# One PSUM accumulator for x, attention and FFN, and another order of the last loads, in a one-token attention and FFN kernel

## The chip, the cores and the metric

The kernel runs on one core of one Trainium2 chip. The metric is the device time of the program in microseconds (us), taken over several executions. A core has a matmul engine (PE, whose weight loads are listed as PEld), a vector engine (DVE), an activation engine (ACT), and a queue processor (SP), which here issues all loads. Sixteen DMA engines carry them out. PE's clock is granted by a throttle and takes two values in these traces, 1.0 and 0.5 of full speed.

All executions quoted here are fast (none was over 1.5% above the fastest of its kernel).

## The reference, cut to what matters

```python
xn = layernorm(x)                                  # x: 4 x 1 x 640, bf16
q  = xn @ wq                                       # 32 heads of 192
scores = q . k_cache[:, :, -2048:, :] * 192**-0.5  # per batch and head
o  = softmax(scores) . v_cache[:, :, -2048:, :]
attention = o @ wo
ffn = (silu(xn @ w1) * (xn @ w3)) @ w2
return x + attention + ffn                         # 4 x 1 x 640
```

K and V of the window are 32 heads x 3.15 MB each, and every byte is used once. With the weights this is 223 MB of loads for an output of 5 KB.

## The kernel before

The kernel walks through 128 slots, four for each head `h`. In each slot DVE multiplies a quarter of the head's K tile by q, PE sums the products in groups with identity matmuls, and DVE reduces what is left. The softmax of a head follows some slots later, then P·V (`pv`), then a regrouping by small matmuls (`ge_tr`, tile `gp`) and, once for four heads, the product with a tile of wo (`ge_proj`). A list of (slot, phase) entries gives every engine its program order. SP issues the loads in that order too, and waits in that order. K tiles have two buffers, V tiles three.

```python
for h in range(H):
    u0, ul = h * GQ, h * GQ + GQ - 1                                  # GQ = 4, H = 32
    if h >= KBUFS:
        add((h - KBUFS + 1) * GQ, 0, load_k, h)                       # K31: slot 120
    add((h - VBUFS) * GQ + GQ + L, 0, load_v, h, 1 if h < H - 1 else 2)   # V29: slot 118
    for u in range(u0, ul + 1):
        add(u, 1, mult, u)                # DVE
        add(u + 1, 2, adder, u)           # PE
        add(u + 2, 4, reduce_quarter, u)  # DVE
    add(u0 + L, 3, pv, h, 0)              # L = 10
    add(u0 + L + 2, 3, pv, h, 1)
    ...                                   # cut: softmax, regrouping
for hg in range(NG):                      # NG = 8 groups of four heads
    a = ((hg + 1) * HG - 1) * GQ + L + 5
    add((hg - 1) * HG * GQ + L + 2 * GQ + 4 if hg > 0 else 0, 0, wo_load, hg)   # wo7: slot 118
    add(a, 3, ge_proj, hg, 0, RPP // 2)
    add(a + 1, 3, ge_proj, hg, RPP // 2, RPP)
...                                       # cut: the FFN up to h, done in the first third
add(NU + 2, 1, w2_load)                   # two pieces, after slot 128
```

The attention is summed in PSUM over all heads (`acc0` with 512 columns, `acc1` with 128). After the last slot the FFN gets its own pair of accumulators, and three addends are joined outside PSUM:

```python
for c, w2 in enumerate(ffn.pop("w2")):    # 12 chunks
    nc.tensor.matmul(f0[:], lhsT=hT[:, c, :], rhs=w2[:, 0:N0], ...)     # 512 columns
    nc.tensor.matmul(f1[:], lhsT=hT[:, c, :], rhs=w2[:, N0:D], ...)     # 128 columns
nc.vector.tensor_copy(out=attn_bf[:, 0:N0], in_=acc0[:])
nc.vector.tensor_copy(out=attn_bf[:, N0:D], in_=acc1[:])
nc.vector.tensor_tensor(out=t1[:], in0=x_sb[:], in1=attn_bf[:], op=ALU.add)
nc.scalar.copy(out=ffn_bf[:, 0:N0], in_=f0[:])
nc.scalar.copy(out=ffn_bf[:, N0:D], in_=f1[:])
nc.vector.tensor_tensor(out=res[:], in0=t1[:], in1=ffn_bf[:], op=ALU.add)
```

Of the kernel before, what the change touches and what calls it, by code (L numbers as in the profile page):

```python
# [10 lines left out]
FP32 = mybir.dt.float32  # L11
BF16 = mybir.dt.bfloat16
ALU = mybir.AluOpType
# [5 lines left out]
def kernel(  # L19
# [20 lines left out]
    nc = tc.nc  # L40
    P = 128
    B, Sq, D = A_x.shape
    _, H, Sk, Dh = A_k_cache.shape
# [3 lines left out]
    FC = F // P  # L47
    PB = P // B
    NJ = W // PB
    GQ = 4  # L50
# [4 lines left out]
    NG = H // HG  # L55
    CT = 32
    QW = HG * Dh
    RPP = QW // P
    NU = H * GQ
    N0 = 512  # L60
    N1 = D - N0
    QC = 512
    NQ = H * Dh // QC
    assert D % P == 0 and F % QC == 0 and P % B == 0 and W % (PB * GQ) == 0
    assert JQ * DD == 512 and JQ % 2 == 0 and 2 * Dh <= 512 and 0 < N1 <= 512
    assert (H * Dh) % QC == 0 and NQ % 6 == 0 and QW % P == 0 and Dh % RPP == 0 and P == HG * CT
    assert 2 * H * Dh <= NJ * Dh

    ctx.enter_context(tc.manual_schedule())
    const = ctx.enter_context(tc.tile_pool(name="const", bufs=1))  # L70
    fpool = ctx.enter_context(tc.tile_pool(name="ffn", bufs=1))
    kpool = ctx.enter_context(tc.tile_pool(name="kt", bufs=KBUFS))
    vpool = ctx.enter_context(tc.tile_pool(name="vt", bufs=VBUFS))
    ppool = ctx.enter_context(tc.tile_pool(name="pr", bufs=PBUFS))
# [4 lines left out]
    ps_m = ctx.enter_context(tc.tile_pool(name="ps_m", bufs=1, space=MemoryType.PSUM))  # L79
    ps_t = ctx.enter_context(tc.tile_pool(name="ps_t", bufs=1, space=MemoryType.PSUM))  # L80
# [28 lines left out]
    x_sb = const.tile([B, D], BF16, name="x_sb")  # L109
# [3 lines left out]
    for k0 in range(0, KC, 2):  # L113
        n = min(2, KC - k0)
        wt = vpool.tile([P, 2, H * Dh], BF16, tag="vt")
        nc.sync.dma_start(out=wt[:, 0:n, :].rearrange("p k n -> p (k n)"),
                          in_=wq_v[:, k0:k0 + n, :].rearrange("p k n -> p (k n)"))
# [4 lines left out]
    idb = const.tile([P, P], BF16, name="idb")  # L122
# [44 lines left out]
    for c0 in range(0, NQ, 6):  # L167
        qps = [pool.tile([P, QC], FP32, tag=tag, name="qps")
               for pool, tag in ((ps_add, "ps"), (ps_add, "ps"), (ps_o, "o_ps"), (ps_o, "o_ps"), (ps_m, "mt"), (ps_t, "t"))]
        for kc in range(KC):  # L170
            for i, qp in enumerate(qps):
                nc.tensor.matmul(qp[:], lhsT=xnT[:, kc].rearrange("p a b -> p (a b)"),  # L172
                                 rhs=wq_rows[kc][:, (c0 + i) * QC:(c0 + i + 1) * QC],
                                 start=(kc == 0), stop=(kc == KC - 1))
# [13 lines left out]

    acc0 = ps_acc.tile([B, N0], FP32, name="acc0")
    acc1 = ps_acc.tile([B, N1], FP32, name="acc1")  # L190

    def mult(u):
        h, g = u // GQ, u % GQ
        pr = ppool.tile([P, JQ, Dh], BF16, tag="pr")
        nc.vector.tensor_tensor(out=pr[:], in0=kts[h][:, g * JQ:(g + 1) * JQ, :],  # L195
                                in1=qbc[:, h * Dh:(h + 1) * Dh].unsqueeze(1).to_broadcast([P, JQ, Dh]),
                                op=ALU.mult)
        prs[u] = pr
        if g == GQ - 1:
            kts.pop(h)  # L200
# [98 lines left out]
    def ge_proj(hg, i0, i1):  # L299
        oT, wo_t = oTs[hg], wos[hg]  # L300
        for i in range(i0, i1):
            st = (hg == 0 and i == 0)
            sp = (hg == NG - 1 and i == RPP - 1)
            nc.tensor.matmul(acc0[:], lhsT=oT[:, i, :], rhs=wo_t[:, i * D:i * D + N0], start=st, stop=sp)  # L304
            nc.tensor.matmul(acc1[:], lhsT=oT[:, i, :], rhs=wo_t[:, i * D + N0:(i + 1) * D], start=st, stop=sp)  # L305

    h_sb = const.tile([B, F], BF16, name="h_sb")
    hT = const.tile([P, FC, B], BF16, name="hT")
    g_bf = const.tile([B, F], BF16, name="g_bf")
    ffn = {}  # L310
# [28 lines left out]
        nc.vector.tensor_copy(out=hT[:], in_=hT_ps[:])  # L339

    w2_v = B_w2.rearrange("(p c) n -> p c n", c=FC)
    W2A = (2 * FC) // 3

    def w2_load():
        wa = fpool.tile([P, W2A, D], BF16, tag="w", name="w2a")
        nc.sync.dma_start(out=wa[:].rearrange("p c n -> p (c n)"), in_=w2_v[:, 0:W2A, :].rearrange("p c n -> p (c n)"))
        wb = kpool.tile([P, FC - W2A, D], BF16, tag="kt", name="w2b")
        nc.sync.dma_start(out=wb[:].rearrange("p c n -> p (c n)"), in_=w2_v[:, W2A:FC, :].rearrange("p c n -> p (c n)"))
        ffn["w2"] = [wa[:, c, :] for c in range(W2A)] + [wb[:, c, :] for c in range(FC - W2A)]

    sched = defaultdict(list)

    def add(slot, phase, fn, *args):
        sched[slot].append((phase, len(sched[slot]), fn, args))

    for h in range(H):
        u0, ul = h * GQ, h * GQ + GQ - 1
        if h >= KBUFS:
            add((h - KBUFS + 1) * GQ, 0, load_k, h)
        add((h - VBUFS) * GQ + GQ + L, 0, load_v, h, 1 if h < H - 1 else 2)  # L360
        for u in range(u0, ul + 1):
            add(u, 1, mult, u)
            add(u + 1, 2, adder, u)
            add(u + 2, 4, reduce_quarter, u)
        add(u0 + L, 3, pv, h, 0)
        add(u0 + L + 2, 3, pv, h, 1)
        add(ul + 2, 5, chain_lmax, h)
        add(ul + 3, 4, chain_tr, h)
        add(ul + 4, 5, chain_gmax, h)
        add(ul + 5, 4, chain_bc, h)  # L370
        add(ul + 6, 5, chain_z, h)
        add(ul + 6, 4, ge_tot, h)
        add(ul + 6, 6, ge_norm, h)
        add(u0 + L + 3, 3, ge_tr, h)
        add(u0 + L + 4, 5, ge_copy, h)
    for hg in range(NG):
        a = ((hg + 1) * HG - 1) * GQ + L + 5
        add((hg - 1) * HG * GQ + L + 2 * GQ + 4 if hg > 0 else 0, 0, wo_load, hg)
        add(a, 3, ge_proj, hg, 0, RPP // 2)
        add(a + 1, 3, ge_proj, hg, RPP // 2, RPP)  # L380
    f = FFN_HEAD * GQ
# [4 lines left out]
    add(f + 12, 7, ffn_up)  # L386
    add(f + 13, 7, ffn_h)
    add(f + 15, 7, ffn_transpose)
    add(NU + 2, 1, w2_load)

    for s in sorted(sched):
        for phase, _, fn, args in sorted(sched[s], key=lambda e: (e[0], e[1])):
            fn(*args)

    f0 = ps_t.tile([B, N0], FP32, tag="t")
    f1 = ps_m.tile([B, N1], FP32, tag="mt")
    for c, w2 in enumerate(ffn.pop("w2")):
        nc.tensor.matmul(f0[:], lhsT=hT[:, c, :], rhs=w2[:, 0:N0], start=(c == 0), stop=(c == FC - 1))  # L398
        nc.tensor.matmul(f1[:], lhsT=hT[:, c, :], rhs=w2[:, N0:D], start=(c == 0), stop=(c == FC - 1))

    attn_bf = ppool.tile([B, D], BF16, tag="pr", name="attn_bf")
    nc.vector.tensor_copy(out=attn_bf[:, 0:N0], in_=acc0[:])
    nc.vector.tensor_copy(out=attn_bf[:, N0:D], in_=acc1[:])
    t1 = ppool.tile([B, D], BF16, tag="pr", name="t1")
    nc.vector.tensor_tensor(out=t1[:], in0=x_sb[:], in1=attn_bf[:], op=ALU.add)
    ffn_bf = ppool.tile([B, D], BF16, tag="pr", name="ffn_bf")
    nc.scalar.copy(out=ffn_bf[:, 0:N0], in_=f0[:])
    nc.scalar.copy(out=ffn_bf[:, N0:D], in_=f1[:])
    res = ppool.tile([B, D], BF16, tag="pr", name="res")
    nc.vector.tensor_tensor(out=res[:], in0=t1[:], in1=ffn_bf[:], op=ALU.add)  # L410
    nc.sync.dma_start(out=out.rearrange("b s d -> (b s) d"), in_=res[:])


# [28 lines left out]
```

## Time and profile before

| | before |
|---|---|
| time, median of 3 runs | 539.77 us |
| span of the profiled run | 538.1 us |
| loads | 223 MB, 421 to 441 GB/s in each stretch of 14 us from 40 to 516 us |
| last K tile (head 31) issued, landed | 483.38, 504.67 us |
| loads over | about 523.3 us |
| DVE busy with head 30 until | 499.82 us |
| last matmul over, store issued, span's end | 534.6, 535.86, 538.1 us |

The first lines to look at are the span and the rows of part 2 of the profile's page: the span cut into 40 slices of 13.45 us, with the busy share of the DMA engines in tenths (9 is 90% or more) and the data rate.

```profile
span 538.1 us, 6726 instructions
...
DMA  8999999999999999999999999999999999999970
GB/s 349 437 427 432 437 427 427 431 431 429 438 435 423 430 435 427 431 436 429 432 433 429 427 434 435 427 429 432 433 432 434 427 436 429 431 426 435 422 305 2
```

The rate is flat from the second slice to the 38th. The Trainium skill, "DMA: Bandwidth & Descriptors", Specifications, gives 435 GB/s as the ceiling of the path into the on-chip memory, and these rates lie on it. As the kernel has to load each byte once, nothing can be gained there. The last slice, however, has next to no loads, and the one before it is not full: the kernel ends with a stretch of pure computing.

The chain of waits that ended last shows where that stretch begins. Its columns are the start, the duration, and what it was.

```profile
483.38 21.29 DMA kt<-in_A_k_cache_dram
504.70 1.76 DVE pr L195
...
535.36 0.48 DVE res L410
```

From the landing of the last K tile at 504.67 us to the end at 538.1 us there are 33.4 us, and no wait on a DMA is in them. The timeline of DVE around that landing tells what DVE did before. The columns are start, duration, engine, line, operation, output and inputs, shapes and count; in brackets stands the idle time before the instruction and what ended it.

```profile
499.61 0.21 DVE L231 TENSOR_SCALAR gneg<-gmax 1x128 f32<-1x128 f32 x1
504.70 1.76 DVE L195 TENSOR_TENSOR pr<-kt,qbc 128x3072 bf16<-128x3072 bf16 x1 [4.87 <-DMA kt<-in_A_k_cache_dram]
...
510.73 0.17 DVE L277 RECIPROCAL rtb<-mt 32x4 f32<-32x4 f32 x1 [0.95 <-PE gp L287]
510.94 1.76 DVE L195 TENSOR_TENSOR pr<-kt,qbc 128x3072 bf16<-128x3072 bf16 x1
```

DVE finished head 30 at 499.82 and waited 4.87 us for the K tile of head 31. This is the most that an earlier K tile can give at this point, however early it comes.

Stretches of time give PE's clock. The columns are the stretch, its length, the busy time of PE, PEld, DVE, ACT and POOL with their instructions, the granted PE clock, the DMA share (some 1.0 is full) and the rate.

```profile
508.00:514.00 6.00, 6.00 (x47) 2.74 (x49) 5.01 (x9) 0.00 (x0) 0.00 (x0) 0.50 0.98 420
...
520.00:524.00 4.00, 3.72 (x75) 2.67 (x78) 1.28 (x5) 0.98 (x4) 0.00 (x0) 1.00 0.37 151
```

PE idles from 503.6 to 507.1 and runs at half clock from about 507.8 to 514.6.

The end itself, from the end of the last matmul to the store:

```profile
534.59 0.57 ACT L407 CAST ffn_bf<-f_4011 4x512 bf16<-4x512 f32 x1 [8.59 <-PE f_4011 L398]
535.07 0.25 ACT L408 CAST ffn_bf<-f_4012 4x128 bf16<-4x128 f32 x1
535.36 0.48 DVE L410 TENSOR_TENSOR res<-t_4040,ffn_bf 4x640 bf16<-4x640 bf16 x1 [3.16 <-ACT ffn_bf L408]
535.86 0.30 SPq L411 DMA_DIRECT2D out_dram<-res  x1
```

Three dependent steps take 1.27 us, from 534.59 to the issue of the store at 535.86.

### The profile page before, as it was taken

How to read it: one execution, taken by the hardware profiler on the slowest of the kernel's cores; microseconds unless marked ns; L12 is line 12 of the kernel's file. 1: busy time of each engine (PE TensorE's matmuls, PEld its weight loads, DVE VectorE, ACT ScalarE, POOL GpSimd, SP SyncE). 2: the span in 40 equal slices, each digit the busy share in tenths (PEclk: the TensorE clock that was granted, in tenths of full speed). 3: DMA queues.
4: the chain of work that ended last, by engine and by line, in shares of the span. 5: the costliest groups of instructions: out<-in, count | busy, mean ns of one | idle time of the engine just before them, and what ended most of it. 6: DMA issues, size and time to landing. Idle time of an engine off the chain costs nothing.

```text
span 538.1 us, 6726 instructions
## 1 busy us (share of the span) xinstructions
PE 380.5 (71%) x2947; PEld 174.2 (32%) x2947; DVE 351.0 (65%) x474; ACT 48.5 (9%) x151; POOL 1.1 (0%) x8
## 2 busy tenths in 40 slices
PE   1765756676687659887767667677677586667796
PEld 0322223332243323333322333333333233333353
DVE  2186777666384756777667757777568657776561
ACT  2111000000132000000000000000000000000010
POOL 0000000000000000000000000000000000000000
PEclk9989789789799996776987998978889998997888
DMA  8999999999999999999999999999999999999970
GB/s 349 437 427 432 437 427 427 431 431 429 438 435 423 430 435 427 431 436 429 432 433 429 427 434 435 427 429 432 433 432 434 427 436 429 431 426 435 422 305 2
DMA packets 11565, 223.39 MB, mean 415 GB/s; under 512 B 1288, under 2 KB 1296, under 8 KB 2448
## 3 DMA queue, kind: packets, MB, share of 16 engines
q1 hardware_dynamic: 11536, 222.97, 96.6%
q8 instruction: 23, 0.38, 0.2%
q14 instruction: 6, 0.05, 0.0%
HBM read 222.96 MB, written 0.01 MB: 414 GB/s over the span
## 4 chain that ended last, share of the span: by engine, by line
DMA 59%; DVE 22%; PE 17%; issue 1%; ACT 1%; SPq 0%; ACTq 0%
DMA kt<-in_A_k_cache_dram 55%; DVE pr L195 16%; PE ps L206 7%; PE gp L287 5%; DVE sc L214 4%; DMA wt<-in_A_wq_dram 4%; PE qps L172 1%; PE gt L322 1%; PE o_ps L259 1%; PE f_4011 L398 1%; DVE rtb L277 0%; PE acc_239 L304 0%; DVE oT L296 0%; DVE qbc L178 0%; ACT o_raw L265 0%
## 5 line engine op out<-in xcount | busy, mean ns | idle before, releaser
L206 PE MATMUL ps<-pr,idb 128*128 128x512 bf16 x768 | 221.3, 433 | 133.6 <-DVE sc L214 129.9
L195 DVE TENSOR_TENSOR pr<-kt,qbc 128x3072 bf16<-128x3072 bf16 x128 | 224.0, 1751 | 107.4 <-DMA kt<-in_A_k_cache_dram 106.3
L206 PEld LDWEIGHTS <-idb 128*128 128x128 bf16 x768 | 78.2, 105 | 228.9 <-issue 171.8
L214 DVE TENSOR_REDUCE sc<-ps 128x16 f32<-128x512 f32 x128 | 87.7, 685 | 8.9 <-PE ps L206 7.9
L259 PE MATMUL o_ps<-vt,z 128*8 128x384 bf16 x1024 | 58.3, 351 | 0.0
L287 PEld LDWEIGHTS gp<-sel,o_raw 128*32 128x32 f32 x768 | 46.8, 151 | 21.4 <-issue 19.8
L265 ACT COPY o_raw<-o_ps 128x384 f32<-128x384 f32 x32 | 15.3, 480 | 408.5 <-PE o_ps L259 408.5
L287 PE MATMUL gp<-sel,o_raw 128*32 128x4 f32 x768 | 49.6, 199 | 1.1 <-ACT o_raw L265 0.6
L259 PEld LDWEIGHTS <-z 128*8 128x8 bf16 x1024 | 20.9, 88 | 39.7 <-issue 31.2
L277 DVE RECIPROCAL rtb<-mt 32x4 f32<-32x4 f32 x32 | 5.7, 178 | 30.3 <-PE gp L287 30.0
L172 PE MATMUL qps<-wt,xnT 128*128 128x512 bf16 x60 | 16.1, 428 | 5.9 <-DMA wt<-in_A_wq_dram 5.9
L178 DVE CAST qbc<-qps 128x512 bf16<-128x512 f32 x6 | 3.8, 685 | 18.8 <-PE qps L172 18.8
L304 PE MATMUL acc_239<-wo_t,oT 128*4 128x512 bf16 x48 | 15.8, 402 | 0.3 <-DVE oT L296 0.3
L250 DVE TENSOR_TENSOR z<-ex,mask_b 128x256 bf16<-128x256 bf16 x32 | 13.4, 418 | 3.0 <-ACT ex L242 3.0
L236 PEld LDWEIGHTS mt<-ones_ff,gneg 1*128 1x128 f32 x64 | 9.4, 182 | 10.2 <-issue 9.9
L236 PE MATMUL mt<-ones_ff,gneg 1*128 1x1 f32 x64 | 12.1, 256 | 0.0
L172 PEld LDWEIGHTS <-xnT 128*128 128x128 bf16 x60 | 6.4, 107 | 15.3 <-issue 9.5
L242 ACT ACTIVATE ex<-sc,negm 128x64 bf16<-128x64 f32 x32 | 11.2, 349 | 1.0
L305 PE MATMUL acc_240<-wo_t,oT 128*4 128x128 bf16 x48 | 11.0, 229 | 0.0
L223 PE MATMUL mt<-idf,lmax 128*1 128x128 f32 x32 | 9.1, 286 | 0.0
L322 PE MATMUL gt<-w_754,xnT 128*4 128x512 bf16 x15 | 6.1, 565 | 4.2 <-DVE oT L296 2.9
L228 DVE TENSOR_REDUCE gmax<-mt 1x4 f32<-1x128 f32 x32 | 8.6, 268 | 0.7 <-PE mt L223 0.7
(61 smaller groups left out, 97.7 us busy)
## 6 DMA issues: line engine op xcount, KB each, us to landing
kt<-in_A_k_cache_dram SPq DMA_DIRECT2D x32, 3072.0 KB, 20.3
vt<-in_A_v_cache_dram SPq DMA_DIRECT2D x31, 3072.0 KB, 24.1
wo_t<-in_A_wo_dram SPq DMA_DIRECT2D x8, 960.0 KB, 25.3
wt<-in_A_wq_dram SPq DMA_DIRECT2D x2, 3072.0 KB, 16.8
vt<-in_A_v_cache_dram SPq DMA_DIRECT2D x2, 1536.0 KB, 14.6
w_754<-in_B_w_dram SPq DMA_DIRECT2D x1, 1920.0 KB, 24.7
w_999<-in_B_w_dram SPq DMA_DIRECT2D x1, 1920.0 KB
wt<-in_A_wq_dram SPq DMA_DIRECT2D x1, 1536.0 KB, 20.0
```

What stands on the lines that cost most here:

```text
L172: nc.tensor.matmul(qp[:], lhsT=xnT[:, kc].rearrange("p a b -> p (a b)"), rhs=wq_rows[kc][:, (c0 + i) * QC:(c0 + i + 1) * QC], start=(kc == ...
L195: nc.vector.tensor_tensor(out=pr[:], in0=kts[h][:, g * JQ:(g + 1) * JQ, :], in1=qbc[:, h * Dh:(h + 1) * Dh].unsqueeze(1).to_broadcast([P, ...
L206: nc.tensor.matmul(ps[:], lhsT=idb[:], rhs=pr[:, :, kk * DD:(kk + 1) * DD], start=(kk == 0), stop=(kk == NK - 1))
L214: nc.vector.tensor_reduce(out=scs[h][:, g * JQ:(g + 1) * JQ], in_=pss.pop(u)[:], axis=AX.X, op=ALU.add)
L236: nc.tensor.matmul(mt[:, P:P + 1], lhsT=gneg[:].rearrange("o p b -> o (p b)"), rhs=ones_ff[0:1, 0:1], start=True, stop=True)
L242: nc.scalar.activation(out=ex[:], in_=scs.pop(h)[:], func=ACTF.Exp, bias=negm[:, 0:1], scale=SCALE, accum_out=rsum[:])
L250: nc.vector.tensor_tensor(out=z[:], in0=ex[:].unsqueeze(2).to_broadcast([P, NJ, B]), in1=mask_b[:].unsqueeze(1).to_broadcast([P, NJ, B]), ...
L259: nc.tensor.matmul(o_ps[c * CT:c * CT + 2 * B, :], lhsT=z[:, 2 * jj:2 * jj + 2, :], rhs=vt[:, 2 * jj:2 * jj + 2, :], start=(jj < 4), stop= ...
L265: nc.scalar.copy(out=o_raw[:].rearrange("q two d -> q (two d)"), in_=o_ps[:])
L287: nc.tensor.matmul(gp[sl, i, :], lhsT=o_raw[:, part, i:Dh:RPP], rhs=sel[:, part * B:(part + 1) * B], start=(part == 0), stop=(part == 1))
L304: nc.tensor.matmul(acc0[:], lhsT=oT[:, i, :], rhs=wo_t[:, i * D:i * D + N0], start=st, stop=sp)
L322: nc.tensor.matmul(gt[:], lhsT=xnT[:, kc, 0, :], rhs=wt[:, kc, n0:n0 + QC], start=(kc == 0), stop=(kc == KC - 1))
```

## The change

The intent is to shorten what follows the last loads. First, x, the attention and the FFN go into one PSUM accumulator, split 320 + 320; x enters by an identity matmul. (The Trainium skill, "PSUM — Partial Sum Buffer", The four PSUM rules, says that a start value other than 0 has to come through PE by an identity matmul, or be added after the copy out of PSUM, and not be written by DVE or ACT. The change does it this way.) Two copies, one on DVE and one on ACT, then end the kernel. Second, the last K tile is issued before V29, and the last wo tile after V31. The diff, cut to its core:

```diff
-    N0 = 512
+    N0 = D // 2
+    def acc_add(lhsT, rhs, first=False, last=False):
+        nc.tensor.matmul(acc0[:], lhsT=lhsT, rhs=rhs[:, 0:N0], start=first, stop=last)
+        nc.tensor.matmul(acc1[:], lhsT=lhsT, rhs=rhs[:, N0:D], start=first, stop=last)
+
+    acc_add(idb[0:B, 0:B], x_sb[:], first=True)
 ...  # ge_proj now calls acc_add; w2 is one tile, loaded by three pieces in place of two tiles
-        add((h - VBUFS) * GQ + GQ + L, 0, load_v, h, 1 if h < H - 1 else 2)
+        add(h * GQ + (2 if h != H - 3 else 5), 0, load_v, h, 1 if h < H - 1 else 2)
-        add((hg - 1) * HG * GQ + L + 2 * GQ + 4 if hg > 0 else 0, 0, wo_load, hg)
+        add(hg * HG * GQ + 8 if hg < NG - 1 else NU, 0, wo_load, hg)
-    add(NU + 2, 1, w2_load)
+    add(NU + 2, 1, w2_load, [(0, FC // 2), (FC // 2, FC - 2), (FC - 2, FC)])
-    f0 = ps_t.tile([B, N0], FP32, tag="t")
-    f1 = ps_m.tile([B, N1], FP32, tag="mt")
 ...  # the FFN's own accumulators, attn_bf, t1 and ffn_bf go
+    for c in range(FC):
+        acc_add(hT[:, c, :], w2[:, c, :], last=(c == FC - 1))
     res = ppool.tile([B, D], BF16, tag="pr", name="res")
-    nc.vector.tensor_tensor(out=res[:], in0=t1[:], in1=ffn_bf[:], op=ALU.add)
+    nc.vector.tensor_copy(out=res[:, 0:N0], in_=acc0[:])
+    nc.scalar.copy(out=res[:, N0:D], in_=acc1[:])
```

The other V tiles keep their slots (4h + 2 in both formulas). The other wo tiles are issued two slots later than before, the first one eight slots later.

More of the change, by code (lines that the diff above doesn't have):

```diff
@@ L66 @@
     assert (H * Dh) % QC == 0 and NQ % 6 == 0 and QW % P == 0 and Dh % RPP == 0 and P == HG * CT
-    assert 2 * H * Dh <= NJ * Dh
+    assert 2 * H * Dh <= NJ * Dh and KBUFS == 2 and VBUFS == 3 and L == 10
     ctx.enter_context(tc.manual_schedule())
@@ L301, in ge_proj @@
         for i in range(i0, i1):
-            st = (hg == 0 and i == 0)
-            sp = (hg == NG - 1 and i == RPP - 1)
-            nc.tensor.matmul(acc0[:], lhsT=oT[:, i, :], rhs=wo_t[:, i * D:i * D + N0], start=st, stop=sp)
-            nc.tensor.matmul(acc1[:], lhsT=oT[:, i, :], rhs=wo_t[:, i * D + N0:(i + 1) * D], start=st, stop=sp)
+            acc_add(oT[:, i, :], wo_t[:, i * D:(i + 1) * D])
     h_sb = const.tile([B, F], BF16, name="h_sb")
@@ L341, with w2_load @@
     w2_v = B_w2.rearrange("(p c) n -> p c n", c=FC)
-    W2A = (2 * FC) // 3
-    def w2_load():
-        wa = fpool.tile([P, W2A, D], BF16, tag="w", name="w2a")
-        nc.sync.dma_start(out=wa[:].rearrange("p c n -> p (c n)"), in_=w2_v[:, 0:W2A, :].rearrange("p c n -> p (c n)"))
-        wb = kpool.tile([P, FC - W2A, D], BF16, tag="kt", name="w2b")
-        nc.sync.dma_start(out=wb[:].rearrange("p c n -> p (c n)"), in_=w2_v[:, W2A:FC, :].rearrange("p c n -> p (c n)"))
-        ffn["w2"] = [wa[:, c, :] for c in range(W2A)] + [wb[:, c, :] for c in range(FC - W2A)]
+    def w2_load(pieces):
+        wt = fpool.tile([P, FC, D], BF16, tag="w", name="w2")
+        for c0, c1 in pieces:
+            nc.sync.dma_start(out=wt[:, c0:c1, :].rearrange("p c n -> p (c n)"),
+                              in_=w2_v[:, c0:c1, :].rearrange("p c n -> p (c n)"))
+        ffn["w2"] = wt
     sched = defaultdict(list)
@@ L393 @@
             fn(*args)
-    f0 = ps_t.tile([B, N0], FP32, tag="t")
-    f1 = ps_m.tile([B, N1], FP32, tag="mt")
-    for c, w2 in enumerate(ffn.pop("w2")):
-        nc.tensor.matmul(f0[:], lhsT=hT[:, c, :], rhs=w2[:, 0:N0], start=(c == 0), stop=(c == FC - 1))
-        nc.tensor.matmul(f1[:], lhsT=hT[:, c, :], rhs=w2[:, N0:D], start=(c == 0), stop=(c == FC - 1))
-    attn_bf = ppool.tile([B, D], BF16, tag="pr", name="attn_bf")
-    nc.vector.tensor_copy(out=attn_bf[:, 0:N0], in_=acc0[:])
-    nc.vector.tensor_copy(out=attn_bf[:, N0:D], in_=acc1[:])
-    t1 = ppool.tile([B, D], BF16, tag="pr", name="t1")
-    nc.vector.tensor_tensor(out=t1[:], in0=x_sb[:], in1=attn_bf[:], op=ALU.add)
-    ffn_bf = ppool.tile([B, D], BF16, tag="pr", name="ffn_bf")
-    nc.scalar.copy(out=ffn_bf[:, 0:N0], in_=f0[:])
-    nc.scalar.copy(out=ffn_bf[:, N0:D], in_=f1[:])
+    w2 = ffn.pop("w2")
+    for c in range(FC):
+        acc_add(hT[:, c, :], w2[:, c, :], last=(c == FC - 1))
     res = ppool.tile([B, D], BF16, tag="pr", name="res")
-    nc.vector.tensor_tensor(out=res[:], in0=t1[:], in1=ffn_bf[:], op=ALU.add)
+    nc.vector.tensor_copy(out=res[:, 0:N0], in_=acc0[:])
+    nc.scalar.copy(out=res[:, N0:D], in_=acc1[:])
     nc.sync.dma_start(out=out.rearrange("b s d -> (b s) d"), in_=res[:])
```

## The prediction

> **What bounds the kernel now.** For most of the span, the loads: the 14 us windows from 40 to 516 us show a DMA share of 0.98 to 1.03 and 421 to 441 GB/s (the Trainium skill, "DMA: Bandwidth & Descriptors", Specifications, puts the fabric ceiling at 435 GB/s; the trace agrees). The change moves the same 223 MB, so this part can't shrink. The loads are over at 523.3 us (half-microsecond windows), the span at 538.1. In the chain of waits the last K tile lands at 504.67 us and 33.4 us follow of compute. No wait on a DMA after 504.67 is in it.
>
> **What the change does.**
> 1. Queue order. Before: K30, V29, wo7, K31, V30, V31, w2. After: K30, K31, V29, V30, V31, wo7, w2. K31 is overtaken by 4.13 MB less, 9.6 us at 430 GB/s, and would land near 495.1 us. Its issue still waits for the last multiply of head 29 (483.36), when K30 is still in flight until 487.92, so I expect no hole in the queue.
> 2. But DVE is not free at 495.1: in the timeline it multiplies head 30 until 498.67 and ends that head's small reductions at 499.82. So the multiply of head 31 starts near 499.8 in place of 504.70: the 4.87 us idle vanishes, not 9.6.
> 3. Part is given back. PE is busy from 499.39 to 503.6 (wo matmuls of group 6, adder, P·V, broadcast), which today fits into the idle time. The next adder starts only at 503.6; 3.0 us later (as from 475.67 to 478.68) DVE gets its reciprocal: its third multiply starts at 506.85, not 510.94. From there I use the durations of head 29 (third multiply to broadcast matmul 7.36 us, full clock): the broadcast of head 30 at 514.2 instead of 518.18, 3.97 us earlier. The half clock of 507.5 to 514.7 should vanish with PE's idle 503.6 to 507.1 (the Trainium skill, "TensorE: Matmul & The Clock Gate", Part 1: about 3.4 us of idleness throttles; the trace shows this after both such gaps); that is counted.
> 4. Late loads: V30 near 509.7, V31 near 517.0, wo7 near 519.3, w2 near 523.5, by bytes at 430 GB/s; needed at about 516, 519.9, 523.9 and 526.8. None should bind.
> 5. The end. Columns per matmul pair stay 640: about 0.27 us as before, so no gain on PE from 320+320. Removed from the chain: the ACT copies of 512 and 128 columns (534.59 to 535.33) and the 0.48 us add, to 535.84; added: two parallel copies of 320 columns, about 0.48 us (between 0.27 and 0.68 us measured for 128 and 512 on DVE). Saves 0.77 us. attn_bf and t1 were hidden; the x seed is free.
>
> **Sum:** 3.97 + 0.77 = 4.7 us: span 533.4, time 539.77 − 4.74 = 535.0 us, range 532.8 to 537.0. Faster by over 2%: 0.04; within 2%: 0.94; slower: 0.02.
>
> **What would show it.** K31 landing near 495 with no DVE wait on it; first multiply of head 31 near 499.8; full clock 500 to 515; a DVE wait of about 1.4 us for the regrouping matmuls; loads over near 523 at an unchanged rate; last copies near 0.5 us.
>
> **What would make it wrong.** A hole in the queue near 485 to 492 or 503 to 507, delaying everything after it; P·V of head 31 or w2 waiting for a DMA; the half clock falling elsewhere in the last 15 us (at 528.2 to 531.6 today, worth up to 1.7 us either way).

## The result, and the profile after

| | before | after |
|---|---|---|
| time, median of 4 runs each | 539.82 us | 534.30 us (534.08 to 535.04) |
| ratio, 95% interval | | 0.9897 (0.9880 to 0.9915) |
| span of the profiled run | 538.1 us | 533.2 us |
| last K tile issued, landed | 483.38, 504.67 | 484.90, 495.9 us |
| head 31's first, third multiply | 504.70, 510.94 | 500.72, 506.90 us |
| last matmul to issue of the store | 1.27 us | 0.44 us |
| loads over | about 523.3 | about 525.5 us |

A ratio is the mean time of one kernel's fast runs over that of the other's fast runs of the same rounds, so it is not quite the ratio of the medians. The change is faster by 1.0%, which counts as the same at a limit of 2%.

The page's first rows after the change:

```profile
span 533.2 us, 6724 instructions
...
DMA  8999999999999999999999999999999999998993
GB/s 353 430 428 431 421 442 424 438 435 428 425 435 432 428 433 431 431 427 439 429 428 431 435 426 438 430 428 435 430 433 428 433 428 440 435 420 372 422 390 140
```

The rate is the same as before until the 37th slice (480 to 493 us), where it dips to 372. The timeline of DVE around the beginning of head 31:

```profile
500.58 0.22 DVE L238 TENSOR_SCALAR gneg<-gmax 1x128 f32<-1x128 f32 x1
500.72 1.74 DVE L202 TENSOR_TENSOR pr<-kt,qbc 128x3072 bf16<-128x3072 bf16 x1
...
506.69 0.18 DVE L284 RECIPROCAL rtb<-mt 32x4 f32<-32x4 f32 x1 [0.90 <-PE gp L294]
506.90 1.76 DVE L202 TENSOR_TENSOR pr<-kt,qbc 128x3072 bf16<-128x3072 bf16 x1
```

The wait on the K tile is gone: DVE goes from head 30 to head 31 without a pause. The tile had been there for almost 5 us, as the list of DMA issues of that stretch shows (KB, and us from issue to landing; the issue was at 484.90):

```profile
kt<-in_A_k_cache_dram SPq DMA_DIRECT2D x1, 3072.0 KB, 11.0
```

So the tile came 8.8 us earlier, and head 31 began 4.0 us earlier. Clock and loads, in stretches with the columns of before:

```profile
482.00:484.00 2.00, 2.00 (x19) 0.42 (x18) 1.94 (x4) 0.00 (x0) 0.00 (x0) 0.56 0.63 270
484.00:486.00 2.00, 1.89 (x13) 0.84 (x10) 1.93 (x4) 0.00 (x0) 0.00 (x0) 1.00 0.41 176
486.00:488.00 2.00, 2.00 (x24) 0.81 (x21) 0.03 (x1) 0.09 (x1) 0.00 (x0) 1.00 0.89 344
...
508.00:514.00 6.00, 4.66 (x47) 1.80 (x46) 5.40 (x9) 0.00 (x0) 0.00 (x0) 1.00 0.95 350
...
520.00:524.00 4.00, 3.14 (x55) 2.44 (x45) 0.51 (x3) 0.48 (x1) 0.00 (x0) 1.00 0.96 401
524.00:528.00 4.00, 4.00 (x20) 2.03 (x18) 0.00 (x0) 0.00 (x0) 0.00 (x0) 0.59 0.11 43
```

Head 31 now runs at full clock (1.00 in place of 0.50 from 508 to 514); the last matmuls still fall into a stretch of half clock (0.59 on average from 524 to 528). But the queue of loads has a hole at 482 to 487: shares of 0.37, 0.59 and 0.11 of 2 us each are missing, 2.1 us in all, while SP stood at the issue of the last K tile and nothing behind K30 was in flight. The loads of this execution end about 2 us later than before. The hole differs between executions: the same sum over 482 to 488 is 0.8 and 1.4 us in the two repetitions below, with the loads over at about 524.2 and 525.0. And the end:

```profile
530.22 0.48 DVE L402 CAST res<-acc_239 4x320 bf16<-4x320 f32 x1 [6.68 <-PE acc_239 L194]
530.36 0.41 ACT L403 CAST res<-acc_240 4x320 bf16<-4x320 f32 x1 [8.65 <-PE acc_240 L195]
530.80 0.30 SPq L404 DMA_DIRECT2D out_dram<-res  x1
```

Two parallel copies in place of three steps in a row. In sum, of the 4.9 us between the two spans, 4.2 us lie before the end of the matmuls and 0.83 us after it; the store itself took 0.16 us longer.

### The profile page after: what moved, and what is told of

Its sections match the earlier page's. It is cut to its first block, busy times and chain, and to the rows that moved or that the text cites. A ratio compares the mean times of both kernels' runs of the same rounds, so it can differ in the third digit from the quotient of the medians.

```text
span 533.2 us, 6724 instructions
## 1 busy us (share of the span) xinstructions
PE 391.0 (73%) x2949; PEld 177.6 (33%) x2949; DVE 349.4 (66%) x471; ACT 48.2 (9%) x150; POOL 1.1 (0%) x8
## 4 chain that ended last, share of the span: by engine, by line
DMA 59%; DVE 22%; PE 17%; issue 1%; ACT 0%; SPq 0%
DMA kt<-in_A_k_cache_dram 56%; DVE pr L202 17%; PE ps L213 7%; PE gp L294 5%; DVE sc L221 4%; DMA wt<-in_A_wq_dram 3%; PE qps L172 2%; PE o_ps L266 1%; PE acc_239 L194 1%; PE acc_240 L195 1%; DVE oT L303 1%; DVE rtb L284 1%; DVE qbc L178 0%; ACT o_raw L272 0%; DVE o_ps L186 0%
## 5 line engine op out<-in xcount | busy, mean ns | idle before, releaser
L213 PE MATMUL ps<-pr,idb 128*128 128x512 bf16 x768 | 228.9, 445 | 119.8 <-DVE sc L221 116.3
L213 PEld LDWEIGHTS <-idb 128*128 128x128 bf16 x768 | 79.5, 108 | 219.8 <-issue 166.7
L172 PE MATMUL qps<-wt,xnT 128*128 128x512 bf16 x60 | 17.7, 463 | 4.9 <-DMA wt<-in_A_wq_dram 4.9
L194 PE MATMUL acc_239<-wo_t,oT 128*4 128x320 bf16 x48 | 13.8, 305 | 0.3 <-DVE oT L303 0.3
L195 PE MATMUL acc_240<-wo_t,oT 128*4 128x320 bf16 x48 | 13.8, 306 | 0.0
```

What stands on the lines that cost most here:

```text
L172: nc.tensor.matmul(qp[:], lhsT=xnT[:, kc].rearrange("p a b -> p (a b)"), rhs=wq_rows[kc][:, (c0 + i) * QC:(c0 + i + 1) * QC], start=(kc == ...
L194: nc.tensor.matmul(acc0[:], lhsT=lhsT, rhs=rhs[:, 0:N0], start=first, stop=last)
L195: nc.tensor.matmul(acc1[:], lhsT=lhsT, rhs=rhs[:, N0:D], start=first, stop=last)
L213: nc.tensor.matmul(ps[:], lhsT=idb[:], rhs=pr[:, :, kk * DD:(kk + 1) * DD], start=(kk == 0), stop=(kk == NK - 1))
```

## The experiments

My theory after the result: the gain is that of the load order, limited by when DVE is free and then by PE, which has to catch up; the accumulator adds only its 0.8 us at the very end; the hole in the queue costs nothing, because neither the last K tile nor the last loads bind. The rivals: that both parts are needed, or the accumulator carries more; that the gain goes with the bytes moved behind the last K tile; that the hole costs its 2 us. There is a further question, whether the clock has a part in the gain. All kernels below gave correct results. The four groups ran on four different chips, each with the kernel before beside it, and each version is compared with the kernel before of its own group. Times are medians of 5 to 7 runs in the same rounds as 9 to 11 runs of the kernel before; those had medians of 538.7, 539.7, 538.5 and 539.7 us in the four groups of runs.

### The changed kernel again

No edit. It ran in two of the groups: that of the accumulator alone, the order alone and V29 first, and that of the second try with PE kept busy and the first two of the last three versions. The versions of the other two groups are compared with it only by their ratios to before.

> The changed kernel once more, for comparison on this chip. Ratio to the kernel before 0.9897 (0.988 to 0.9915) as measured at first, about 534.2 us; the profile again shows a thin DMA share for some microseconds around the issue of the last K tile, with no wait of DVE on that tile.

Measured: 532.98 us, ratio 0.9884 (0.9862 to 0.9907). As expected.

> The changed kernel in the same rounds, as the yardstick for the two versions that try to beat it: ratio to before 0.988 to 0.990.

Measured: 533.43 us, ratio 0.9904 (0.9883 to 0.9925). As expected. The three ratios, 0.9897, 0.9884 and 0.9904, are the yardstick for the rest.

### The accumulator alone, and the order alone

```diff
 # accumulator alone: the changed kernel, with the loads in the order of before
-        add(h * GQ + (2 if h != H - 3 else 5), 0, load_v, h, 1 if h < H - 1 else 2)
+        add((h - VBUFS) * GQ + GQ + L, 0, load_v, h, 1 if h < H - 1 else 2)
-        add(hg * HG * GQ + 8 if hg < NG - 1 else NU, 0, wo_load, hg)
+        add((hg - 1) * HG * GQ + L + 2 * GQ + 4 if hg > 0 else 0, 0, wo_load, hg)
-    add(NU + 2, 1, w2_load, [(0, FC // 2), (FC // 2, FC - 2), (FC - 2, FC)])
+    add(NU + 2, 1, w2_load, [(0, 8), (8, FC)])
```

> Only the single accumulator (x, attention and FFN in one PSUM sum, two parallel copies at the end); every load in the order of before. My theory: the accumulator is worth only what it takes off the end of the chain, 0.8 us (1.27 us from the last matmul to the store's issue before, 0.44 after): about 539.0 us, the last K tile lands near 504.7 again with about 4.9 us idle on DVE. Rival: the accumulator gives a large part of the 5.5 us (fewer PSUM hand-overs, another clock at the end): 537 us or less.

Measured: 539.32 us, ratio 1.0008 (0.9983 to 1.0033). In the profile the last K tile is waited for again, as the theory said:

```profile
504.67 1.76 DVE L202 TENSOR_TENSOR pr<-kt,qbc 128x3072 bf16<-128x3072 bf16 x1 [4.67 <-DMA kt<-in_A_k_cache_dram]
```

The rival is out: the accumulator does not carry the gain. Its own 0.8 us (a ratio of 0.9985) lies inside the interval and is not resolved by the time. (The profiled run, 536.73 us, is the fastest of this kernel: in it the clock stayed at 1.00 from 499 us to the end.)

```diff
 # order alone: the changed kernel, with N0 = 512, no x in PSUM, f0/f1, attn_bf, t1, ffn_bf as before
-    N0 = D // 2
+    N0 = 512
-    acc_add(idb[0:B, 0:B], x_sb[:], first=True)
-            acc_add(oT[:, i, :], wo_t[:, i * D:(i + 1) * D])
+            acc_add(oT[:, i, :], wo_t[:, i * D:(i + 1) * D], first=..., last=...)
 ...  # and the end of the kernel before
```

> Only the load order; separate accumulators, three ACT and DVE steps at the end as before. My theory: about 4.0 to 4.7 us below before, so 535.1 to 535.8 us; head 31's first multiply near 500.7 without a wait on its K tile; 1.2 to 1.3 us from the last matmul to the store. Rival (both parts are needed together): less than 3 us.

Measured: 533.68 us, ratio 0.9895 (0.9873 to 0.9918), so some 5.6 us below before, more than the 4.0 to 4.7 expected. The order carries all of the gain that the times can resolve. The profiles of this run and of the first repetition of the changed kernel agree to 0.1 us from the first multiply of head 31 (498.89 and 498.98 us) to the last regrouping (523.03 and 522.99 us), so they isolate the accumulator. The end of the timeline, order alone:

```profile
529.58 0.30 SPq L415 DMA_DIRECT2D out_dram<-res  x1
```

and the changed kernel, repeated:

```profile
528.76 0.30 SPq L404 DMA_DIRECT2D out_dram<-res  x1
```

The store is issued 0.82 us earlier, and the spans are 531.9 and 531.1 us. That is the accumulator's share.

### V29 before the last K tile again

```diff
-        add(h * GQ + (2 if h != H - 3 else 5), 0, load_v, h, 1 if h < H - 1 else 2)
+        add(h * GQ + 2, 0, load_v, h, 1 if h < H - 1 else 2)
```

> The changed kernel with V tile 29 issued before the last K tile again, wo still after V31. The last K tile is then overtaken by 3.15 MB, 7.3 us at 430 GB/s, and should land near 502.4 us, no thin DMA share near 482 to 487. My theory: the K tile may come as late as 500.7 without cost, because DVE works on head 30 until then; so this loses only about 1.5 to 2.2 us against the changed kernel (536 us). Rival (the gain is that of bytes moved behind the last K tile): loses 7.3/9.6 of the gain of the order, 3 us or more (537.3 us or more).

Measured: 535.90 us, ratio 0.9940 (0.9914 to 0.9965), against 0.9884 of the changed kernel in the same rounds: 0.0056, or 3.0 us lost. The median met the rival's "3 us or more" and not the theory's 1.5 to 2.2, but from the two intervals I estimate this difference only to some 1.2 to 4.8 us, so the times don't decide between the two. The profile speaks for the theory. DVE, this kernel:

```profile
502.50 1.76 DVE L202 TENSOR_TENSOR pr<-kt,qbc 128x3072 bf16<-128x3072 bf16 x1 [3.52 <-DMA kt<-in_A_k_cache_dram]
...
507.93 0.17 DVE L284 RECIPROCAL rtb<-mt 32x4 f32<-32x4 f32 x1 [0.34 <-PE gp L294]
508.13 1.76 DVE L202 TENSOR_TENSOR pr<-kt,qbc 128x3072 bf16<-128x3072 bf16 x1
```

and the changed kernel, repeated in the same group:

```profile
498.98 1.74 DVE L202 TENSOR_TENSOR pr<-kt,qbc 128x3072 bf16<-128x3072 bf16 x1
...
506.33 0.18 DVE L284 RECIPROCAL rtb<-mt 32x4 f32<-32x4 f32 x1 [1.70 <-PE gp L294]
506.54 1.76 DVE L202 TENSOR_TENSOR pr<-kt,qbc 128x3072 bf16<-128x3072 bf16 x1
```

The K tile landed at 502.5 as computed from bytes, and head 31 began 3.5 us later than in the changed kernel. Yet its third multiply came only 1.6 us later, because the changed kernel waits longer for PE there (1.70 against 0.34 us, with another 0.49 us on ACT). The spans of these two profiled runs differ by 1.6 us. Starting DVE earlier than PE can follow is given back within two multiplies: this is the step of the prediction called "given back", seen by itself. As to the other 1.4 us of the difference in time: the profiled run is the fastest of this kernel (534.50 of 534.50 to 537.11), while the changed kernel's runs lie closer (531.93 to 533.52). In both profiles PE has full clock from head 31 on, so this part isn't in them. It pointed to the clock, and to the next but one experiment, but no trace of a slow run of this version shows it.

### The last wo tile before the last K tile: the hole filled

```diff
-        add(hg * HG * GQ + 8 if hg < NG - 1 else NU, 0, wo_load, hg)
+        add(hg * HG * GQ + 8 if hg < NG - 1 else (H - 3) * GQ + 2, 0, wo_load, hg)
```

> The changed kernel with the last wo tile (0.98 MB) issued before the last K tile: it fills the thin stretch of the queue (DMA share 0.25 to 0.77 between 482 and 487 in the changed kernel's profile). My theory: the thin stretch costs nothing, because the last K tile has some 5 us to spare and the loads at the end some 2 us; so the time stays that of the changed kernel within 0.5 us (ratio to before 0.988 to 0.990), while the loads end about 1 to 2 us earlier. Rival: the hole pushes back what follows it, so filling it gains 1.5 us or more (ratio 0.986 or less).

Measured: 533.41 us, ratio 0.9901 (0.9875 to 0.9927). In the profile the hole is mostly gone; stretches of this kernel:

```profile
482.00:484.00 2.00, 2.00 (x21) 0.61 (x20) 1.94 (x4) 0.00 (x0) 0.00 (x0) 0.69 0.98 420
484.00:486.00 2.00, 1.70 (x9) 0.71 (x8) 1.81 (x4) 0.00 (x0) 0.00 (x0) 1.00 0.83 355
...
522.00:524.00 2.00, 1.72 (x26) 1.49 (x26) 0.19 (x1) 0.00 (x0) 0.00 (x0) 1.00 0.48 195
```

The changed kernel's DMA share at 522 to 524 was 0.94 in its first profile; here it is 0.48. But the loads end at about 524.6, so 0.8 us before those of that profile and no earlier than in the repetition (524.2): the forecast of 1 to 2 us was missed. The time is that of the changed kernel within the interval of 1.4 us either way. (This profile is of one of the two slow runs, 534.98 us; its clock is 0.50 from about 524.2 to 527.6.) The test is also not a clean one, as the wo tile now stands before V31, and PE waited 0.16 us for V31's second half. That the hole cost the changed kernel nothing rests more on its own profile: the chain that ended last has no wait on a DMA after the landing of K30 at 488.50, and K30 had been issued at 470.80, well before the hole.

### PE kept busy in the kernel before

```diff
 # in adder(u) of the kernel before, first try
+        for _ in range(14 if u == (H - 1) * GQ else 0):
+            nc.tensor.matmul(ps[:]..., lhsT=idb[:], rhs=qbc[:, 0:QC], start=True, stop=True)
```

> The kernel before with 14 extra 128x512 matmuls (about 3.0 us, results overwritten) on PE while it waits for the last K tile, so that PE is not idle there; loads and everything else as before. My theory: part of the gain of the load order is the clock: PE's idle time before the last head, gone after the change, lets the clock fall to 0.5 in some executions. Then this kernel keeps full clock through head 31, is 0.5 to 1.3 us faster than before by its median, and its slowest runs come down more than its fastest. Rival (the clock plays no part in the gain): within 0.3 us of before, with the same spread (537.2 to 540.9).

Measured: 543.54 us, ratio 1.0076 (1.0045 to 1.0107), a failed experiment. The timeline of PE shows why:

```profile
507.04 4.87 PE L206 MATMUL ps<-qbc,idb 128*128 128x512 bf16 x14 [3.54 <-DVE sc L216]
```

The bank I wrote to was freed by a reduction that stands behind the multiply in DVE's order, so the extra matmuls began after the wait that they should have filled, and delayed the last head. The second try took a bank that was free:

```diff
+        if u == (H - 1) * GQ:
+            dm = ps_t.tile([P, QC], FP32, tag="t", name="dm")
+            for _ in range(14):
+                nc.tensor.matmul(dm[:], lhsT=idb[:], rhs=qbc[:, 0:QC], start=True, stop=True)
```

> The kernel before with the 14 extra matmuls again, now into a PSUM bank that is free, so that they run from about 503.6 to 506.6 us, while PE waits for the last K tile (in the first try they waited for a bank that DVE freed only at 507.0, ran after it and delayed the last head by 4.7 us). My theory: with PE not idle before head 31 the clock stays full through that head; 0.5 to 1.3 us faster than before by the median, and the slow end of its spread comes down. Rival (the clock plays no part): within 0.3 us of before, same spread.

Measured: 537.37 us, ratio 0.9977 (0.9954 to 1.0001), so about 1.2 us with an interval that just reaches 1: the rival, no more than 0.3 us, is not excluded by the times. PE's timeline and a stretch of this kernel:

```profile
503.50 3.19 PE L208 MATMUL dm<-qbc,idb 128*128 128x512 bf16 x13
```

```profile
508.00:510.00 2.00, 2.00 (x30) 1.56 (x29) 1.73 (x4) 0.00 (x0) 0.00 (x0) 1.00 0.95 406
```

(The trace holds 13 of the 14 matmuls; a few records can be missing.) The clock stays at 1.00 through head 31, where before had 0.50. The single runs say more than the mean. The 11 runs of before in this group lie in four clusters: 537.1 to 537.2 (three), 538.4 to 538.5 (three), 539.5 to 539.7 (four) and 540.5 (one). With PE kept busy there are two: 537.15 to 537.38 (four) and 539.0 to 539.1 (two). This fits two separate events of half clock, one in head 31 and one in the last matmuls, of which the extra matmuls took away the first. Two timed runs have a trace. That of before at the start (539.91 us) has both events, in head 31 and from 528.3 to 531.7; that of this kernel (539.02 us, in its upper cluster) has only the second, at the same time and as long. Their spans, 538.1 and 537.2 us, put the first event at 0.9 us, and this kernel's two clusters, if the lower one has neither event, put the second at about 1.8. The other runs have no trace, so the reading of the clusters is argued, not shown, and the run of 540.5 stays unexplained. The clock would explain why the change gave 5.2 to 6.3 us by its three ratios (one minus the ratio, times 539 us), and 4.9 us between the first two profiles.

### K30 before V28 as well

```diff
-        add(h * GQ + (2 if h != H - 3 else 5), 0, load_v, h, 1 if h < H - 1 else 2)
+        add(h * GQ + (5 if H - 4 <= h <= H - 3 else 2), 0, load_v, h, 1 if h < H - 1 else 2)
```

> The changed kernel with V tile 28 moved behind K tile 30 as well. My theory: what bounds the end now is the chain that starts when K tile 30 lands, with DVE idle 2.5 to 3.3 us before it; K30 lands 7.3 us earlier by bytes, but DVE is free only at the end of head 29, so the gain is that idle, 2.5 to 3.2 us against the changed kernel, and V28 fills the hole around the issue of the last K tile. About 529.8 to 530.5 us, ratio to before 0.983 to 0.985. If instead the loads of V31, wo and w2 bind (they end near 523.5), the gain is 1 us or less.

Measured: 534.13 us, ratio 0.9905 (0.9879 to 0.9931): no gain. It was the second branch. Head 30 began without a wait (484.70), and DVE was 4.5 us ahead of the repeated changed kernel at the end of head 30 (515.35 against 519.80). Then PE waited for V31:

```profile
519.15 1.45 PE L266 MATMUL o_ps<-vt,z 128*8 128x384 bf16 x16 [2.85 <-DMA vt<-in_A_v_cache_dram]
...
523.01 0.43 PE L194 MATMUL acc<-wo_t,oT 128*4 128x320 bf16 x1 [0.28 <-DVE oT L303]
```

The end had changed its bound, from the computing chain to the loads. The clock was 0.50 from about 516.1 to 526.2 us; it fell 0.2 us before PE began to wait for V31's second half (at 516.30), so that wait is not what lowered it. There was a new hole in the queue as well, at 468 to 474 us (DMA share 0.54, 0.73, 0.81), since nothing but the rest of K29 was in flight when SP waited to issue K30.

### Three versions that build on it

The first gives the queue half of V28 to work on while SP waits for K30's buffer:

```diff
+        if h == H - 4:
+            add(h * GQ + 2, 0, load_v, h, 2, 0)      # first half of V28
+            add(h * GQ + 5, 0, load_v, h, 2, 1)      # second half
+        else: ...
```

> As the version with K30 before V28, but only the second half of V28 is behind K30; the first half stays before it and should fill the hole of about 1.8 us (DMA share 0.54 to 0.81 from 468 to 474) that delayed V31, for whose second half PE waited 2.85 us. Theory: head 30 still starts without a wait near 484.5, V31 lands about 1.8 us earlier (near 517.4), and the end comes 1.5 to 2 us before that of the version with K30 first: about 532 us, ratio 0.986 to 0.988. Rival (V31 comes no earlier, or the half clock at the end takes it): ratio 0.989 to 0.991.

Measured: 534.41 us, ratio 0.9913 (0.9892 to 0.9934). In the profiles V31 came 1.5 us earlier than with K30 first (PE's wait for it ended at 517.67 in place of 519.15), and the span was 1.1 us shorter, but the profiled run was the fastest of this kernel, and the times show no gain. By the times the rival holds. That the half clock took what V31 gained is argued only: it was 0.50 from 515.3 to 525.5 us here, but with K30 first as well.

The second adds matmuls without use while PE waits, six before the second half of P·V of head 31 and two behind it:

```diff
+    def warm(n):
+        dm = ps_add.tile([P, QC], FP32, tag="ps", name="dm")
+        for _ in range(n):
+            nc.tensor.matmul(dm[:], lhsT=idb[:], rhs=qbc[:, 0:QC], start=True, stop=True)
 # in pv(h, half)
+        if h == H - 1 and half == 1:
+            warm(6)
 ...  # the matmuls of P·V, and the copy of their result by ACT
+            if h == H - 1:
+                warm(2)
```

> The version with V28 split, and eight extra 128x512 matmuls on PE while it waits for V31 and for the copy after its P·V. Theory: the last wo and w2 matmuls ran at half clock from 523 to 526 (0.27 us each, 0.135 at full clock), because PE idles while waiting for V31; kept busy, they run at full clock: 1.5 us or more off, about 530.5 us, ratio 0.983 to 0.985. Rival: the clock doesn't follow such short work: as the split version.

Measured: 531.98 us, ratio 0.9862 (0.9837 to 0.9887), against 0.9913 without these matmuls in the same rounds: 0.0051, about 2.7 us from eight matmuls of 1.8 us in all (from the two intervals I estimate 1.0 to 4.5 us). PE's timeline without them:

```profile
521.54 0.43 PE L194 MATMUL acc<-wo_t,oT 128*4 128x320 bf16 x1 [0.28 <-DVE oT L303]
521.76 0.47 PE L195 MATMUL acc<-wo_t,oT 128*4 128x320 bf16 x1
522.03 0.47 PE L194 MATMUL acc<-wo_t,oT 128*4 128x320 bf16 x1
```

and with them:

```profile
522.27 0.30 PE L194 MATMUL acc<-wo_t,oT 128*4 128x320 bf16 x1 [0.28 <-DVE oT L312]
522.41 0.30 PE L195 MATMUL acc<-wo_t,oT 128*4 128x320 bf16 x1
522.54 0.30 PE L194 MATMUL acc<-wo_t,oT 128*4 128x320 bf16 x1
```

The steps from one start to the next are 0.13 to 0.14 us in place of 0.22 to 0.27: full clock in place of half. The gain was larger than the 1.5 us that I had expected as a minimum, but the time stayed 1.5 us above the 530.5 forecast. That these matmuls kept the clock up is not shown by this pair: without them it fell at about 515.3, 0.2 us after PE began to wait (515.07), and with them the first began only 0.16 us into the wait, so they could hardly have prevented that fall. What the traces show is full clock in all of the last matmuls with them, here and in the next version.

The third puts a quarter of V29 before the last K tile, to fill the hole at 482 to 486 too:

```diff
+        elif h == H - 3:
+            add(h * GQ + 2, 0, load_v, h, 4, 0)      # first quarter of V29
+            for i in range(1, 4):
+                add(h * GQ + 5, 0, load_v, h, 4, i)
```

> The version with V28 split and the eight extra matmuls, with the first quarter of V29 (0.79 MB, 1.8 us) issued before the last K tile as well, to fill the thin stretch of 482 to 486 (DMA share 0.75 and 0.54 there, some 1.2 us lost). Theory: V31, which the end now waits for, lands about 1 us earlier; 0.5 to 1.2 us off, ratio to before 0.984 to 0.986. Rival (the last K tile now comes too late, or V31 doesn't come earlier): as before or slower, 0.986 to 0.989.

Measured: 530.55 us (530.44 to 530.95), ratio 0.9829 (0.9815 to 0.9843). DVE waits for the last K tile, but P·V of head 31 finds its V tile there, with no wait on a DMA (in the version before this one PE waited 1.09 us, until 519.04):

```profile
497.51 1.76 DVE L202 TENSOR_TENSOR pr<-kt,qbc 128x3072 bf16<-128x3072 bf16 x1 [1.09 <-DMA kt<-in_A_k_cache_dram]
...
518.12 0.82 PE L273 MATMUL o_ps<-vt,z 128*8 128x384 bf16 x16
```

This is the fastest version: 1.7% below before (still "the same" at a limit of 2%), and 0.55 to 0.75% below the changed kernel by their ratios, from other groups. The same split without the extra matmuls was not run. The fastest version needs eight matmuls that compute nothing.

## Why the prediction was right

It gave 535.0 us (532.8 to 537.0), within 2%; measured were 534.3 us, and 532.98 and 533.43 in the repetitions, all inside the range.

1. "The loads can't shrink": right. The rate was the same outside the hole, and the span fell only at its end.
2. "DVE is not free at 495.1": right, and the decisive step. The last K tile landed at 495.9 (495 forecast), 8.8 us earlier, and head 31 began 3.98 us earlier in that profile. The forecast start was 499.8; it was 500.72 in the first profile, where K30 itself had landed 0.6 us later and head 30 ran partly at half clock, and 498.98 in the repetition.
3. "Part is given back": right. The third multiply was forecast for 506.85 and came at 506.90, and at 506.54 in the repetition, although the two had started 1.7 us apart. The wait for the regrouping matmuls was 0.90 and 1.70 us around the forecast 1.4. The experiment with V29 in its old place shows the same limit from the other side.
4. The broadcast matmul of head 30 was forecast for 514.2 and came at 513.90.
5. The end: 0.77 us forecast, 0.83 measured; order alone against the whole change gives 0.82.
6. "I expect no hole in the queue": wrong. There was one of 2.1 us of full load time in the first profile, 0.8 and 1.4 in the repetitions. I took the landing of K30 (487.92) as the time until which the queue is busy. But a tile has landed when its last part has, and the DMA engines don't end together: their mean share was 0.69 at 482 and 0.25 at 485. Its forecast consequence, "delaying everything after it", did not come, as the chain of the first profile shows and the test with the wo tile moved agrees with: the last K tile had 4.8 us to spare and the last loads more than one.
7. "Loads over near 523": they ended at about 525.5, later by about the size of this hole, and at 524.2 and 525.0 in the repetitions.
8. The size: the forecast of 4.74 us stands against 5.5 by the first medians and 5.2 to 6.3 by the ratios. Between the two profiled executions (the forecast was worked out from the first) it was 4.9, so there the terms fit. That the medians differ more I put down to the clock, which is argued, as most runs have no trace. The prediction said of the half clock in head 31 that it "is counted", without a figure of its own; the profiles with PE kept busy and without give 0.9 us for it (by time about 1.2, interval from 0 to 2.5). The half clock in the last matmuls, which the prediction named as a risk of up to 1.7 us, was in the first profile of the changed kernel (at 535.04 us the slowest of its four runs) and not in the repetition's. That the median lay so near the forecast is in part luck.

## What to carry to other kernels

When a load is to come earlier, look up when the engine that uses it is free: the gain is the smaller of the two, and then ask whether the next engine in line can follow (here 8.8 us of load time became 4.0 us). A kernel at the end of its loads changes its bound with every microsecond gained: computing first, then the last V tile, and, as far as the times tell, PE's clock; moving more loads gained nothing here until matmuls without use kept PE busy in its waits. A queue that issues in order needs something in flight while it stands at a wait, and "landed" tells only when the slowest part is done; a part of a later tile, put before the wait, fills the hole.

## What the Trainium skill lacked or had wrong

- "DMA: Bandwidth & Descriptors", Where 436 GB/s comes from, says that for transfers from HBM the limit of about 358 GB/s per core binds. That sentence lacks a condition, which the same page gives under its table of measured sizes, where it marks 425 GB/s as a number of a single core. Here one core alone read HBM at 421 to 441 GB/s for over 470 us, at the ceiling of 435 that the same page gives for the other side (421 to 441 are means of 14 us, so a little above it is within the reading).
- No page that I used gives a figure for how far apart the sixteen DMA engines end one queue's work: the share of before was about half for 4.6 us (518.7 to 523.3) at the end, and this spread opened the hole at 482 us while the tile counted as in flight.
- "TensorE: Matmul & The Clock Gate", Part 1, has the clock fall after about 3.4 us of idleness. The trace of before agrees (idle from 503.6 to 507.1 us, then 0.50), but the length of one gap did not decide it here: the clock had fallen by 490.6 in the first profile of the changed kernel, 2.4 us into a gap, and it stayed at 1.00 after gaps of 2.92 us (accumulator alone) and 3.00 us (V29 first).
- The same page describes, under "A second HAM failure mode: psum-queue depth-cycling", for matmuls of 512 columns that cycle through PSUM banks, that short idle times between groups of matmuls let the clock swing. What it lacks is how little idleness is enough: from 520 to 524 us PE was busy 3.14 of 4 us, with matmuls that move 4 columns among them, and the clock was 0.50 from 524.8 to 528; in the repetition the same matmuls, with the same busy time, ran on at 1.00. Nor has it a figure for how much work in a wait keeps the clock up, and the runs here don't settle it: with eight matmuls of 128x512 (1.8 us in all) in the waits the last matmuls had full clock in both profiles, and the first of the two versions gained 0.0051 in the ratio.
